# Turning the second group's queries on TensorE at the head of a fused attention and ELU kernel

## The chip, the cores and the metric

The kernel runs on one core of a Trainium2 chip. The metric is the time of one execution in microseconds, as the median over several runs. A core has a matrix engine (TensorE, PE in the profile, with its weight loads shown apart as PEld), a vector engine (VectorE, DVE), a scalar engine (ScalarE, ACT), a general engine (GpSimd, POOL) and a queue engine that issues most DMAs (SyncE, SP). Each engine works through its own instructions in order and waits on semaphores for the others.

## The reference

Everything is float32. The first part is an attention with a polynomial feature map, the second a two-layer network with an ELU:

```python
# q, k, v: (4, 4, 1088, 32); S1, S2: (8, 32)
def phi(x):
    a = np.einsum('rd,bhsd->bhsr', S1, x)
    b = np.einsum('rd,bhsd->bhsr', S2, x)
    return np.einsum('bhsi,bhsj->bhsij', a, b).reshape(*x.shape[:-1], 64)
q_p, k_p = phi(q), phi(k)
kv = np.einsum('bhsf,bhsd->bhfd', k_p, v)
z = np.sum(k_p, axis=2)
num = np.einsum('bhsf,bhfd->bhsd', q_p, kv)
den = np.einsum('bhsf,bhf->bhs', q_p, z)[..., None] + 1e-06
x = (num / den).transpose(0, 2, 1, 3).reshape(4352, 128)

# w_in: (128, 2048), w_out: (2048, 128)
h = x @ w_in
g = np.where(h > 0.0, h, np.exp(np.minimum(h, 0.0)) - 1.0)
out = g @ w_out
```

## The kernel before

**Tiles and groups.** A batch has 17 tiles of 64 tokens, so there are 68 in all. Eight tiles make a group, g = 0 to 8. Group 0 is tiles 0 to 7 of batch 0, group 1 is tiles 8 to 15 of batch 0; tile 16 of batch 0 belongs to group 2. `x` of a group lies transposed in SBUF as `xg` (128 features by 512 tokens). The network's 2048 middle columns are taken in eight chunks cp of 256. For each pair (g, cp), `mm1` makes `h` in two halves, `elu_a` (ACT) and `elu_d` (DVE) turn it into `gg`, and `mm2` adds up the output. Groups 2 to 7, and the last chunks of group 1, use a scheme of seven products in place of eight for `mm2` (`sums7` on POOL, `mm2_seven` on PE); it isn't touched.

**Loads.** Inputs arrive as pairs of 32-bit words, and the weights are rounded on the chip to float32 by the steps RA, RB, RC (RS, RM, RD) and RE, all of which are on DVE but RB, which is on ACT (line 106). RC_2 does RS, RM and RD of the first two blocks at once. The queries of a batch come into `hd_q` with heads and 32 token groups on the partitions. For batch 0 they come in two DMAs, tiles 0 to 7 and tiles 8 to 16.

**The head.** The program is written out by hand in the order in which every engine is to see its instructions (`manual_schedule`). The head brings the first group to `mm1`:

- `transp` (line 281, DVE) turns blocks of 32 by 32 of `hd_q` or `hd_k` into `qT` or `kT`, where the feature dimension is on the partitions.
- `KF`, `KO_pool` and `KO_first` make the key features, `KA` (line 428) adds up `kv` over the tiles. `KS_first` copies `kv` twice side by side (kd, ACT), turns it on PE, and copies the result to `kvS` (ACT).
- `q1_first`, `q1z_first`, `q2_den` and `q2_out` make the first group's query features `qp` on DVE, with RA(0) and RA(1) in between.
- `q4_early` (line 636) turns `qp` on PE in two halves of two heads, through PSUM tiles `qtp`, and ACT copies each half into `qpT` (line 637).
- `q1_second` (line 537) multiplies the second group's `qT` with `SW`, which holds the two feature matrices and the sums z; ACT copies the result into `abw` (line 541), and q2(1) later makes the second group's features from it.
- `q5_early` (line 643) multiplies `qpT` with `kvS` in 16 small tiles into two PSUM tiles `xps`, one for each half w of the token columns; ACT copies them into `xg` (line 649).
- `mm1_first` (line 857) does the first `mm1` column half by column half, so that it can start when the first of the two copies is there.
- `keep_warm` issues matmuls on constants whose result nobody reads.

Matmuls with fewer than 128 output columns sit in parts of the array; `tile_position` says which. A float32 matmul shows in the profile as two records. PSUM tiles come from rings: `h` has four banks, `aux` two, `o0` and `o1` one each.

After the head, a loop over `steps` runs `mm1`, the ELU and `mm2` of a step two back. Other work is hung onto steps by `at` (behind `mm1`), `mid` and `late` (behind the ELU).

## Time and profile before

| | |
|---|---|
| median of 3 runs | 265.38 us (265.32 to 265.83) |
| the profiled execution | 265.08 us |
| its span, first to last instruction | 263.3 us |
| TensorE's granted clock | 1.000 |
| DMA in the first 25 us | 176 to 349 GB/s in most slices |
| stretch 0 to 9.40 us | PE busy 8.29, DVE 6.67, ACT 3.11 |
| stretch 9.40 to 15.55 us | PE busy 5.16, DVE 5.73, ACT 3.62 |
| stretch 15.55 to 18.30 us | PE busy 2.72, DVE 2.65, ACT 1.64 |

The profile is one execution. Times in it count from the first instruction. A row of a timeline reads: start, length, engine, line, operation, output and inputs, shapes, count, and in brackets the idle time before it and what ended that. A row with a count covers several instructions, from the first one's start to the last one's end. Rows of the chain read: start, length, what.

### The profile page before, as it was taken

The numbers are of one execution on the slowest core, as the hardware profiler recorded it, in microseconds if no ns is written. First come the engines' busy times: TensorE is split into PE (matmuls) and PEld (weight loads), VectorE is DVE, ScalarE is ACT, GpSimd is POOL, SyncE is SP. The second block draws the span as 40 slices with busy tenths as digits, with TensorE's granted clock in tenths as the row PEclk, the third lists the DMA queues.
The fourth block names the chain that finished last, engine by engine and source line by source line (L and its number), as shares of the span: only waits on it lengthen the run. The fifth ranks groups of instructions, "written<-read, shape, count | busy, mean of one in ns | idle before, by whom it ended". The sixth has DMA issues, their size and how long they took to land.

```text
span 263.3 us, 9739 instructions
## 1 busy us (share of the span) xinstructions
PE 257.8 (98%) x4127; PEld 160.5 (61%) x4127; DVE 188.2 (71%) x349; ACT 184.5 (70%) x356; POOL 168.2 (64%) x251
## 2 busy tenths in 40 slices
PE   8899999999999999999999999999999999999994
PEld 7652334354346756667666666665666666667994
DVE  6899999997969997996477676644446445674651
ACT  2479978677567656775587777776777777777793
POOL 4400009105477996798869799888688888998300
PEclk9999999999999999999999999999999999999999
DMA  5997099020011110000100110011001100110011
GB/s 176 339 349 209 2 277 230 1 72 18 2 24 26 26 20 2 2 4 17 31 3 0 29 18 0 2 19 25 3 2 21 23 4 0 18 20 8 2 30 32
DMA packets 26442, 13.73 MB, mean 52 GB/s; under 512 B 19328, under 2 KB 24576, under 8 KB 26400
## 3 DMA queue, kind: packets, MB, share of 16 engines
q1 hardware_dynamic: 25968, 12.76, 18.9%
q8 instruction: 32, 0.52, 0.9%
q10 hardware_dynamic: 368, 0.30, 0.3%
q0 software_dynamic: 64, 0.07, 0.1%
q14 instruction: 10, 0.08, 0.1%
HBM read 10.88 MB, written 2.23 MB: 50 GB/s over the span
## 4 chain that ended last, share of the span: by engine, by line
PE 96%; POOL 1%; DVE 1%; ACT 1%; issue 0%
PE h L257 44%; PE pb L792 16%; PE pa L792 13%; PE o L257 5%; PE pb L768 4%; PE ol L257 3%; PE idle L265 1%; PE kv L428 1%; PE h L686 1%; PE qps L686 1%; POOL kp L324 1%; PE kfps L360 1%; PE qps L576 1%; PE qtp L636 1%; PE kv L257 1%; PE abp L341 1%
## 5 line engine op out<-in xcount | busy, mean ns | idle before, releaser
L257 PE MATMUL h<-xg,W 128*32 128x512 f32 (+3 forms) x904 | 130.7, 539 | 0.4 <-ACT xg L649 0.4
L875 DVE SCALAR_TENSOR_TENSOR gg<-e,h 128x512 f32<-128x512 f32 x128 | 85.6, 683 | 54.1 <-ACT e L869 50.6
L867 ACT ACTIVATE e<-h 128x512 f32<-128x512 f32 x128 | 75.5, 590 | 45.6 <-PE h L257 42.9
L869 ACT ACTIVATE e<-e 128x512 f32<-128x512 f32 x128 | 80.9, 632 | 3.8
L257 PEld LDWEIGHTS h<-xg,W 128*32 128x32 f32 (+1 forms) x904 | 42.6, 122 | 43.2 <-issue 34.9
L754 POOL TENSOR_TENSOR tt<-gg 128x256 f32<-128x256 f32 x50 | 37.0, 741 | 16.4 <-DVE gg L875 16.1
L751 POOL TENSOR_TENSOR tt<-gg 128x256 f32<-128x256 f32 x50 | 36.7, 734 | 5.5 <-DVE gg L875 5.1
L755 POOL TENSOR_TENSOR tt<-tt,gg 128x256 f32<-128x256 f32 x50 | 37.5, 750 | 3.9
L756 POOL TENSOR_TENSOR tt<-gg,tt 128x256 f32<-128x256 f32 x50 | 37.2, 744 | 3.9
L792 PEld LDWEIGHTS pa<-gg,W 128*64 128x64 f32 (+1 forms) x496 | 23.8, 125 | 23.5 <-issue 22.9
L792 PE MATMUL pa<-gg,W 128*64 128x128 f32 (+1 forms) x496 | 30.5, 274 | 0.0
L792 PE MATMUL pb<-tt,SS 128*64 128x128 f32 (+1 forms) x480 | 29.5, 273 | 0.0
L792 PEld LDWEIGHTS pb<-tt,SS 128*64 128x64 f32 (+1 forms) x480 | 22.6, 126 | 0.0
L792 PE MATMUL pa<-tt,SS 128*32 128x128 f32 (+1 forms) x288 | 21.0, 273 | 0.0
L133 POOL TENSOR_TENSOR raw<-raw,tiny 128x512 f32<-128x512 f32 x1 | 1.0, 1044 | 29.4 <-DVE raw L128 29.4
L792 PE MATMUL pb<-tt,W 128*64 128x128 f32 (+1 forms) x256 | 19.8, 273 | 0.0
L792 PE MATMUL pb<-gg,SS 128*64 128x128 f32 (+1 forms) x256 | 19.8, 273 | 0.0
L257 PE MATMUL o<-gg,W 128*32 128x512 f32 x128 | 15.3, 594 | 0.0
L792 PEld LDWEIGHTS pa<-tt,SS 128*32 128x32 f32 (+1 forms) x288 | 13.6, 124 | 0.0
L792 PEld LDWEIGHTS pb<-gg,SS 128*64 128x64 f32 (+1 forms) x256 | 12.7, 125 | 0.0
L792 PEld LDWEIGHTS pb<-tt,W 128*64 128x64 f32 (+1 forms) x256 | 12.6, 125 | 0.0
L768 PE MATMUL pb<-gg,W 128*32 128x256 f32 x192 | 11.5, 380 | 0.0
(163 smaller groups left out, 279.5 us busy)
## 6 DMA issues: line engine op xcount, KB each, us to landing
raw<-in_moe_w_in_dram SPq DMA_DIRECT2D x8, 256.0 KB, 6.6
raw<-in_moe_w_out_dram SPq DMA_DIRECT2D x8, 256.0 KB, 6.4
hd_k<-in_k_dram SPq DMA_DIRECT2D x3, 544.0 KB, 7.3
hd_q<-in_q_dram SPq DMA_DIRECT2D x3, 544.0 KB, 7.9
out_dram<-ob SPq DMA_DIRECT2D x88, 16.0 KB, 1.5
v<-in_v_dram SPq DMA_DIRECT2D x4, 288.0 KB, 6.8
v<-in_v_dram SPq DMA_DIRECT2D x4, 256.0 KB, 8.3
hd_k<-in_k_dram SPq DMA_DIRECT2D x1, 288.0 KB, 3.3
```

Source lines behind the costliest of these rows:

```text
L257: nc.tensor.matmul(dst[c:c + tile], lhs[:, c:c + tile], rhs, skip_group_check=True, tile_position=(0, c), **kw)
L265: nc.tensor.matmul(idle[c:c + tile, :cols], ones[:, :tile], ones[:, :cols], skip_group_check=True, tile_position=(0, c))
L686: nc.tensor.matmul(ps[w][s * r:s * r + s, 64 * k:64 * (k + m)], lhs, qpT[g, i][rows, o + 2 * k:o + 2 * (k + m), f, :], start=(f == 0 and j ...
L751: nc.gpsimd.tensor_tensor(t[:, 0], b12, b11, op=SUB)
L754: nc.gpsimd.tensor_tensor(t[:, 2], b22, b12, op=SUB)
L755: nc.gpsimd.tensor_tensor(t[:, 1], t[:, 2], b11, op=ADD)
L756: nc.gpsimd.tensor_tensor(t[:, 3], b21, t[:, 1], op=SUB)
L768: nc.tensor.matmul(acc[1][0][r:r + width[0], 256 * hi:256 * hi + 256], lhs[:, w:w + width[0]], gg[:, c, 256 * u:256 * u + 256], start=(cp ...
L792: nc.tensor.matmul(bank[r:r + width[0], P * col:P * col + P], lhs[:, w:w + width[0]], rhs[:, u], start=(first and i in ((0,) if g == 1 els ...
L867: nc.scalar.activation(e, hs[g, cp][c][:, :n], RELU, scale=-1.0)
L869: nc.scalar.activation(e, e, EXP, scale=-1.0)
L875: nc.vector.scalar_tensor_tensor(gs[g, cp][:, c, :n], es[g, cp][:, c, :n], -1.0, hs[g, cp][c][:, :n], op0=ADD, op1=MAX)
```

## The change

DVE no longer turns the second group's queries in one instruction between the first group's features and the rounding of the weights. Instead `turn_q` multiplies each 32 by 32 block with the identity on PE, in four tiles on the diagonal of the array, and `turn_q_out` copies the result on ACT to `qT`. This happens in two batches of four query tiles behind `KA`, in one PSUM bank, with the first part of `KS_first` in between. Tile 16 is still turned by DVE, behind step 3 of the loop. RB(0) moves ahead of `KA`; RB(1) stands behind the second copy. `KS_first`'s copy to `kvS` moves into `q4_early` between its two halves. `q1_second` is split into three parts: one between the halves of `q4_early`, one between the two pairs of heads of `q5_early`, and one behind them. Its copy to `abw` stands between the two copies to `xg`. The second `xps` tile of group 0 comes from the ring of `h` in place of `aux`. One `keep_warm` goes, another shrinks from 192 columns to 64.

```diff
--- before.py
+++ after.py
@@ -281,6 +281,23 @@
         nc.vector.transpose(dst[b][:, t0:t1, :].rearrange("p t (a c) -> p c t a", c=2), hd[x, b][:, :, t0:t1, :])
 
 
+
+    def turn_q(t0, t1):
+        if not turned_q:
+            turned_q.append(psum.tile([P, 512], F32, name="qtu", tag="h", bufs=4))
+        for t in range(t0, t1):
+            for c in range(2):
+                for h in range(H):
+                    r = slice(D * h, D * h + D)
+                    o = 64 * (t - 8) + 32 * c
+                    nc.tensor.matmul(turned_q[0][r, o:o + 32], hd["q", 0][r, c, t, :], ident[r, r],
+                                     skip_group_check=True, tile_position=(D * h, D * h))
+
+    def turn_q_out(t0, t1, copy=nc.scalar.copy):
+        copy(qT[0][:, t0:t1, :].rearrange("p t (a c) -> p t a c", c=2),
+             turned_q[0][:, 64 * (t0 - 8):64 * (t1 - 8)].rearrange("p (t c a) -> p t a c", c=2, a=32))
+
+    turned_q = []
     SXh = const.tile([P, FD], F32, name="SXh")
 
     def make_SXh():
@@ -475,10 +492,12 @@
             z_tile(0, ps, i)
         return ps, ZC(0, ps)
 
-    def KS_first():
+    def KS_first_a():
         kd = work.tile([P, 2, R * R], F32, name="kd", tag="kd", bufs=1)
         nc.scalar.copy(kd[:], _ap(kv_ps[0][:, :R * R], [[0, 2], [1, R * R]]))
         nc.tensor.transpose(kv_ps[0][:, 128:256], kd[:].rearrange("p w f -> p (w f)"), ident[:])
+
+    def KS_first_b():
         nc.scalar.copy(kvS[:].rearrange("p h d -> p (h d)"), kv_ps[0][:, 128:256])
 
     def KV_first():
@@ -529,14 +548,21 @@
                                  qT[b][:, t, :], SW[:, :, 2, :], skip_group_check=True, tile_position=(0, 64 * u))
         return p[:, :128].rearrange("p (t h r) -> p h t r", t=4, h=H)
 
-    def q1_second():
-        p = psum.tile([P, 512], F32, name="abwp", tag="h", bufs=4)
-        for i in range(4):
+    second = []
+
+    def q1_second(i0, i1):
+        if not second:
+            second.append(psum.tile([P, 512], F32, name="abwp", tag="h", bufs=4))
+        p = second[0]
+        for i in range(i0, i1):
             for u in range(2):
                 b, t = half_tile(1, 2 * i + u)
                 nc.tensor.matmul(p[64 * u:64 * u + 64, i * 96:i * 96 + 96], qT[b][:, t, :],
                                  SW[:].rearrange("p h x r -> p (h x r)"), skip_group_check=True,
                                  tile_position=(0, 64 * u))
+
+    def q1_second_out():
+        p = second[0]
         abw[1] = work.tile([P, H * 4, 3 * R], F32, name="abw1", tag="abq1", bufs=1)
         nc.scalar.copy(abw[1][:].rearrange("p (h t) y -> p h t y", h=H),
                        p[:, :384].rearrange("p (t h y) -> p h t y", t=4, h=H))
@@ -624,7 +650,7 @@
             nc.vector.tensor_mul(qp[g][:, h], _ap(a_, list(a_.ap[1:]) + [[0, R]]),
                                  _ap(b_, [b_.ap[1], [0, R], b_.ap[2]]))
 
-    def q4_early(g):
+    def q4_early(g, between=None):
 
         qpT[g] = work.tile([P, H, 2, P], F32, name="qpT", tag="qpT", bufs=2)
         for hh in range(2):
@@ -635,18 +661,32 @@
                     r = (2 * hh + h2) * 4 + 2 * m
                     nc.tensor.transpose(p[:, o:o + P], qp[g][:, r:r + 2].rearrange("p t i j -> p (t i j)"), ident[:])
             nc.scalar.copy(qpT[g][:, 2 * hh:2 * hh + 2], p[:].rearrange("p (h m s) -> p h m s", h=2, m=2))
+            if between and hh == 0:
+                between()
 
     def q5_early(g):
-        xp = [psum.tile([P, 512], F32, name="xps", tag="aux") for _ in range(2)]
-        for h in range(H):
+        q5_early_a(g, range(H))
+        q5_early_b(g)
+
+    def q5_early_a(g, hs_):
+        if 0 in hs_:
+            xps[g] = [psum.tile([P, 512], F32, name="xps", **kw) for kw in
+                      (dict(tag="aux"), dict(tag="h", bufs=4) if g == 0 else dict(tag="aux"))]
+        xp = xps[g]
+        for h in hs_:
             for w in range(2):
                 nc.tensor.matmul(xp[w][D * h:D * h + D, :256], kvS[64 * w:64 * w + 64, h, :],
                                  qpT[g][64 * w:64 * w + 64, h].rearrange("p m s -> p (m s)"),
                                  skip_group_check=True, tile_position=(64 * w, D * h))
+
+    def q5_early_b(g, between=None):
+        xp = xps.pop(g)
         xg[g] = work.tile([P, 512], F32, name="xg", tag="xg", bufs=3)
         to = xg[g][:].rearrange("p (m w s) -> p w m s", w=2, s=P)
         for w in range(2):
             nc.scalar.copy(to[:, w], xp[w][:, :256].rearrange("p (m s) -> p m s", s=P))
+            if between and w == 0:
+                between()
 
 
     def heads(g):
@@ -965,19 +1005,24 @@
     zq = q1z_first()
     q2_den(0, zq, lambda: RA(0))
     q2_out(0, 2, lambda: RA(1))
+    RB(0)
     KA(0)
-    KS_first()
-    keep_warm(1)
-    RB(0)
+    turn_q(8, 12)
+    KS_first_a()
+    turn_q_out(8, 12)
+    turn_q(12, 16)
+    turn_q_out(12, 16)
     RB(1)
-    q4_early(0)
-    transp(qT, "q", 0, 8, NT)
+    q4_early(0, lambda: (KS_first_b(), q1_second(0, 1)))
     RC_2()
     RE(0)
     RE(1)
-    q1_second()
-    q5_early(0)
-    keep_warm(1, 192, width[0])
+    q5_early_a(0, (0, 1))
+    q1_second(1, 3)
+    q5_early_a(0, (2, 3))
+    q1_second(3, 4)
+    q5_early_b(0, q1_second_out)
+    keep_warm(1, 64, width[0])
     mm1_first()
     q2(1, 2, lambda: RA(2))
     RB(2)
@@ -1065,6 +1110,7 @@
         late(n_a, sums_out, b)
         at(n_z, turn, b)
         late(n_z, turned, b)
+    late(3, transp, qT, "q", 0, 16, NT)
     late(10, transp, qT, "q", 1, 0, NT)
     at(21, transp, qT, "q", 2, 0, NT)
     late(24, transp, qT, "q", 3, 0, NT)
```

## The prediction

> **What bounds the kernel now.** I read the page's busy shares first, then its chain of waits, then the same chain in order of time for the first 50 us, and last the timeline and single tiles there.

> ```profile
> PE 257.8 (98%) x4127; PEld 160.5 (61%) x4127; DVE 188.2 (71%) x349; ACT 184.5 (70%) x356; POOL 168.2 (64%) x251
> ...
> PE 96%; POOL 1%; DVE 1%; ACT 1%; issue 0%
> ```

> TensorE is busy 98% of the span and carries 96% of the chain: whatever starts its dense part later makes the kernel that much longer. The chain in order of time shows where the dense part starts (start, length, what):

> ```profile
> 11.01 0.69 DVE qp L624
> 11.70 0.21 DVE W L101
> 11.91 0.61 DVE qp L624
> 12.52 0.14 issue
> 12.65 0.63 PE qtp L636 x4
> 13.28 0.85 PE abwp L537 x16
> 14.13 0.70 PE xps L643 x16
> 14.83 0.64 ACT xg L649 x2
> 15.47 0.11 issue
> 15.58 2.79 PE h L257 x40
> ```

> From 15.58 (`mm1_first`) on only PE rows follow. So the change is worth what it does to 15.58, plus what its side effects do soon after. The timeline of that stretch (start, length, engine, line, tiles, count, idle before):

> ```profile
> 7.50 0.16 PEld L419 LDWEIGHTS zps<-abk 128*32 128x32 f32 x8 [0.22 <-ACT abk L349]
> 9.43 1.21 PE L428 MATMUL kv<-kp,v 128*32 128x64 f32 x72
> 10.71 0.27 ACT L480 COPY kd<-kv 128x128 f32<-128x128 f32 x1 [1.90 <-PE kv L428]
> 11.55 0.91 ACT L106 ACTIVATE W<-W,ebias 128x256 uint32<-128x256 uint32 x2
> 12.42 0.77 DVE L281 STREAM_TRANSPOSE qT<-hd_q 128x576 f32<-128x576 f32 x1
> 12.45 0.59 ACT L637 COPY qpT<-qtp 128x512 f32<-128x512 f32 x1
> 13.31 0.59 ACT L637 COPY qpT<-qtp 128x512 f32<-128x512 f32 x1 [0.28 <-PE qtp L636]
> 14.18 0.48 ACT L541 COPY abw<-abwp 128x384 f32<-128x384 f32 x1 [0.27 <-PE abwp L537]
> 15.01 0.76 DVE L136 SCALAR_TENSOR_TENSOR W<-raw,W 128x256 f32<-128x256 f32 x2
> ```

> Two strands meet at 15.58. One is x: `qpT`, `xps`, then `xg`, whose first pair of columns is copied by about 15.18. The other is W: DVE's transposition (12.42 to 13.19), then RC_2, then RE(0), whose first instruction ends at 15.43. PE takes 0.115 us from a DVE end to a load behind two waits (12.50 to 12.62 at the second `qtp`), so 15.43 + 0.115 is 15.55, where the load of `h` stands. The chain names ACT, but x had been there for 0.3 us: W came last. Taking 0.77 us off DVE there looks like a gain.

> [...] here records of different tiles start 7 ns apart (below). [...] the pair at 11.55 overlaps by 0.10 (two of 0.51 and 0.50 in 0.91).

> **The change part by part.** *Turning.* One `turn_q` call issues 4 tiles x 2 x 4 = 32 matmuls, and an f32 matmul is two records (KA: 36 matmuls, 72 records), so 64, on four tiles of the array at a time. Not in the trace; bounds: eight loads of 0.109 in 0.16 us start 7 ns apart, so at least 64 x 7 ns = 0.45; KA's 72 records with twice the columns take (1.21 - 0.22) / 72 = 13.8 ns each, so at most 0.88. I take 8 ns, 0.51, near the lower end since half as many columns stream, and add the 0.20 that one record of 32 columns lasts (`zps`, 196 ns): 0.71. Changing the tile's shape costs PE the stream of the last record and about 0.09 (last `abwp` record at 13.88, first `xps` at 14.06: 96 columns at 0.84 ns, then 0.09; last `qtp` to `h`: 0.2 for 128 columns).

> *The new order*, with 0.05 from an engine's end to the next engine's start (kd to its transposition: 10.98 to 11.03):

> - PE: KA's last record starts at 10.42; `turn_q(8, 12)` 10.57 to 11.28. Its data, the second half of the first `hd_q`, completes in the trace at 10.39, so 0.18 is spare; SP's queue is unchanged there. kd's transposition follows at 11.2.
> - ACT: RB(0) moves to 10.2 to 10.7, where ACT was idle 1.90 us: free. kd is copied to 10.98 as before. First copy-out, 128x256 from PSUM, 0.37 (like `abq` and `xg`): 11.33 to 11.70.
> - PE: `turn_q(12, 16)` writes the bank that this copy reads, so it waits: 11.75 to 12.46. Queued behind it on PE are `qtp` and all that x needs. ACT: second copy 12.51 to 12.88.
> - ACT: RB(1), now behind this copy, 12.78 to 13.29 (before: ended 12.46). DVE's RC_2 waits for RB(1): 13.35 instead of 13.12. The removed 0.77 us become 0.85 us of waiting; RE(0) ends at 15.67, 0.24 later.
> - PE: first `qtp` four 12.38 to 13.04 (before 11.76 to 12.41), first part of `q1_second`, second `qtp` four 13.27 to 13.90.
> - ACT: `qpT` 13.19 to 13.78, kvS to 13.94, `qpT` to 14.53 (before 13.90).
> - PE: first two heads of x from 13.99, their second records 0.24 later; `q1_second(1, 3)` 14.56; last two heads 15.04 to 15.68. In before, x ended at 14.72. Two shape switches, 0.3 each with the streams, lie in front of the last heads: features between the heads aren't free.
> - ACT: first `xg` copy 15.75 to 16.12; `abw` copy to 16.51; second `xg` copy to 16.79, in time for `mm1_first`'s second half (16.17 + 4 x 0.215 = 17.03).
> - PE: `mm1_first` at 16.17: **+0.59**.

> *After that.* q2(1) on DVE waits for `abw`: 16.57 instead of 15.68, +0.89. Its `qp` ends at 19.22; the second `qtp` four of the second group would want it at 19.38: just hidden. But DVE runs without a break from 17.03 to 22.9, so RE(2), which ended at 20.73, ends 0.82 later, and mm2(0, 0) starts at 21.60 instead of 20.91. That makes +0.69. Beyond, DVE rounds and ELUs have 0.8 us or more before PE needs them (RE(3) ends at 23.84 for 26.09), so it neither grows nor is won back.

> *Costed at nothing*: the smaller `keep_warm`s (they fill PE's idle time; no cover needed); tile 16's transposition at step 3 (0.2 us like other small ones, in DVE's slack behind 26; without that, +0.2); `hd_q`'s later release (the load that reuses it is issued at 34.73, after step 3 near 28; SP's later loads stand behind it); the fifth to eleventh `h` tiles (their readers are done by then); POOL has no part.

> **Sum**: +0.7. The profiled execution took 265.08 us (span 263.3 and 1.8 around it), so it would be about 265.8; the median of the runs is 265.38, 0.3 higher, so **266.1**.

> **Unknown costs.** Turning: 0.45 to 0.88 each, -0.1 to +0.74 for both, since the two are in line. Bank wait: 0, if hardware order allowed it, to the 0.42 taken; without it -0.35. Shape switches: hidden to as priced, -0.35 to 0. DMA: if the half landed with w_out's delay of 6.4 instead of 5.8, 10.95, +0.4; I take 10.39.

> **Rivals.**
> 1. *Little change*: second turn isn't held by the first copy, or switches overlap; x is then +0.0 to +0.35, and W +0 (RB(1) at 12.94 at the latest). For: PE had 1.1 us of idle time between 10.64 and 11.76. About 265.6.
> 2. *Turning at KA's rate*: +0.7 + 0.74, 266.8. For: the tiles stay loaded only 32 columns, and each needs its own weight load. Against: loads run ahead.
> 3. *Faster*: DVE's freed time is used. RC_2 could start at 12.56, when `qp` ends, so W could be ready at 15.0: -0.55, 264.8. It decides where the second copy-out ends by 12.1, so that RB(1) ends by 12.5, and x is out of PSUM by 15.0. For: W is the last strand today. Against: the second copy waits for turn, copy, turn in sequence; even at 7 ns a record it ends at 12.8.
> 4. *Clock*: with less warming PE drops to a lower clock for some us, +1 to +2. Against: PEclk is 9 in all slices and PE's longest new gap is about 0.6 us.

> **Chances.** Forecast 0.55 (0.10 of it under the bound), rival 1 0.16, rival 2 0.17, rival 3 0.08, rival 4 0.04. A difference under 0.2%, 0.53 us, can't be told from none. So slower 0.45 + 0.17 + 0.04 = 0.66, same 0.26, faster 0.08. The forecast's own range is 265.6 to 266.6; with rivals 1 and 2 most of the way, 265.2 to 267.0.

> **What would show it.** In the profile after: 64 `qtu` records a call in about 0.7 us; the second batch starting 0.05 behind the first copy's end at about 11.7; RC_2's first instruction waiting on ACT `W` near 13.3; `xg` ending near 16.1 and 16.8; `h` starting at 16.2 and `o` at 21.6. It is wrong if `qtu` is one unbroken batch, if RB(1) ends by 12.5, or if `h` starts by 15.6.

## The result, and the profile after

The changed kernel takes **271.58 us** (median; 271.34 to 272.18) against 265.39 for the kernel before on the same chip: ratio 1.0231, 95% interval 1.0214 to 1.0247. The sign was forecast, the size was not: +6.2 us where +0.7 was expected, far above the range's upper end of 267.0. Of the 6.2 us only about 0.5 came by the way that was forecast (few_records, below). The profiled execution spans 270.0 us, 6.7 more than before.

The rows of the page (busy time and share, chain by engine, granted clock in 40 slices of 6.75 us):

```profile
span 270.0 us, 9994 instructions
PE 261.9 (97%) x4253; PEld 162.9 (60%) x4253; DVE 188.0 (70%) x349; ACT 185.4 (69%) x358; POOL 168.3 (62%) x251
PEclk9959999999999999999999999999999999999999
PE 95%; issue 1%; DMA 1%; ACT 0%; DVE 0%; SPq 0%; DVEq 0%
```

PE has 126 matmul records more: 128 of the two turning calls, less 2 of the `keep_warm` that went. As many weight loads come with them (PEld, x4253 against x4127). Two things are new. "issue" has 1% of the chain, and in the third slice the clock stands at 5, half speed. The chain of waits in order of time (start, length, what) shows both:

```profile
9.68 1.21 PE kv L445 x72
10.89 0.53 PE qtu L293 x37
11.42 3.14 issue
14.56 0.56 PE qtu L293 x21
15.12 0.02 issue
15.14 0.38 ACT qT L297
15.52 0.04 issue
15.57 1.07 PE qtu L293 x64
16.64 1.04 PE qtp L662 x4
17.69 0.52 PE abwp L560 x4
18.21 1.05 PE qtp L662 x4
...
22.23 2.70 PE h L257 x40
```

In the middle of the first turning call PE does nothing for 3.14 us, and no semaphore is behind it: "issue" is time in which the engine waited for nothing that the profile shows. The timeline gives the same in records:

```profile
10.86 0.56 PE L293 MATMUL qtu<-ident,hd_q 32*32 32x32 f32 x43
14.56 0.54 PE L293 MATMUL qtu<-ident,hd_q 32*32 32x32 f32 x21 [3.14 <-issue]
15.57 1.07 PE L293 MATMUL qtu<-ident,hd_q 32*32 32x32 f32 x64
22.14 2.79 PE L257 MATMUL h<-xg,W 128*32 128x256 f32 x40
```

43 of the call's 64 records run, then the engine stops between two instructions of one kind, on one tile, with its inputs there (the call's queries came in one DMA). The second call of 64 takes 1.07 us, and the `qtp` fours take 1.04 and 1.05 in the chain instead of 0.63. The windows of that time (start:end, length, busy us and count of PE, PEld, DVE, ACT, POOL, then the granted clock, DMA share, GB/s) say why:

```profile
10.81:14.23 3.42, 0.61 (x50) 0.48 (x43) 1.78 (x4) 0.29 (x2) 0.00 (x0) 1.00 1.08 372
14.23:17.64 3.41, 3.01 (x92) 2.26 (x92) 0.12 (x1) 1.15 (x3) 0.00 (x0) 0.50 1.08 374
17.64:21.05 3.41, 3.41 (x28) 1.82 (x28) 2.46 (x5) 1.34 (x3) 0.00 (x0) 0.50 1.08 276
21.05:24.47 3.42, 3.42 (x62) 1.68 (x60) 1.83 (x6) 2.30 (x6) 0.00 (x0) 1.00 1.01 288
```

Behind 3.42 us in which PE was busy for only 0.61, the clock is at half for 6.83 us. `h` starts at 22.14 instead of 15.58, 6.56 late, and the span is 6.7 longer: nearly all of the loss lies ahead of `h`.

### The profile page after: what moved, and what is told of

Same layout as the page of the kernel before. It is cut to its first block, busy times and chain, and to the rows that moved or that the text cites. A ratio compares the mean times of both kernels' runs of the same rounds, so it can differ in the third digit from the quotient of the medians.

```text
span 270.0 us, 9994 instructions
## 1 busy us (share of the span) xinstructions
PE 261.9 (97%) x4253; PEld 162.9 (60%) x4253; DVE 188.0 (70%) x349; ACT 185.4 (69%) x358; POOL 168.3 (62%) x251
## 4 chain that ended last, share of the span: by engine, by line
PE 95%; issue 1%; DMA 1%; ACT 0%; DVE 0%; SPq 0%; DVEq 0%
PE h L257 43%; PE pb L832 16%; PE pa L832 13%; PE o L257 5%; PE pb L808 4%; PE ol L257 3%; PE kv L445 2%; DMA hd_k<-in_k_dram 1%; PE h L726 1%; PE qtp L662 1%; PE qps L726 1%; PE xps L678 1%; PE qtu L293 1%; PE abp L358 1%; PE kfps L377 1%
## 5 line engine op out<-in xcount | busy, mean ns | idle before, releaser
L257 PE MATMUL h<-xg,W 128*32 128x512 f32 (+3 forms) x904 | 130.7, 540 | 0.0
L257 PEld LDWEIGHTS h<-xg,W 128*32 128x32 f32 (+1 forms) x904 | 42.4, 122 | 42.8 <-issue 34.9
L794 POOL TENSOR_TENSOR tt<-gg 128x256 f32<-128x256 f32 x50 | 37.0, 741 | 16.2 <-DVE gg L915 15.9
L832 PEld LDWEIGHTS pa<-gg,W 128*64 128x64 f32 (+1 forms) x496 | 23.8, 125 | 23.5 <-issue 22.9
L257 PE MATMUL o<-gg,W 128*32 128x512 f32 x128 | 15.3, 594 | 0.0
L832 PEld LDWEIGHTS pb<-gg,SS 128*64 128x64 f32 (+1 forms) x256 | 12.6, 125 | 0.0
```

The costliest lines, as they stand in the source:

```text
L257: nc.tensor.matmul(dst[c:c + tile], lhs[:, c:c + tile], rhs, skip_group_check=True, tile_position=(0, c), **kw)
L794: nc.gpsimd.tensor_tensor(t[:, 2], b22, b12, op=SUB)
L832: nc.tensor.matmul(bank[r:r + width[0], P * col:P * col + P], lhs[:, w:w + width[0]], rhs[:, u], start=(first and i in ((0,) if g == 1 els ...
```

## The theories

**The theory: PE ran out of instructions.** The page has a DMA queue for instructions, q8. These are its rows (packets, MB, share), first before, then after:

```profile
q8 instruction: 32, 0.52, 0.9%
q8 instruction: 33, 0.54, 0.9%
```

In the trace each of its packets has 16,384 bytes (what a packet brings is called a block below), and the kernel with more PE instructions has one packet more: 32 for 8,254 loads and matmuls before, 33 for 8,506 after. The first packet of the span runs from 12.06 to 13.16 us in this kernel, and PE goes on 1.4 us behind it. Counting PE's loads and matmuls from the start, the stop comes after record 442. The kernel before reaches its 442nd record at 14.35 and starts its 443rd at 14.65, in the first of these rows (the second is from few_records, an experiment below):

```profile
14.65 0.16 PEld L265 LDWEIGHTS idle<-const-float32-1.0 128*32 128x32 f32 x8 [0.41 <-issue]
14.48 0.51 PEld L558 LDWEIGHTS abwp<-SW,qT 128*64 128x64 f32 x8 [0.41 <-issue]
```

The 0.30 us between the two records of before aren't a stop: the same 0.30 lies behind `xps` in few_records, where record 442 is still to come. So before, the next block of instructions came in time, though not by much: its 443rd record starts 1.56 us behind the end of the packet. Each turning call adds 64 loads and 64 matmul records in some 0.5 us, and PE comes to the end of the instructions at hand 3.1 us earlier (record 442 at 11.23 instead of 14.35), while the packet ends when it did before (13.16 against 13.09).

**The rivals.** Something in the turning itself holds PE: its data, its PSUM bank, or the array's tiles. Or the new order costs more than was worked out, and the clock with it. A second question was why the block comes so late: because PE asks late, or because the DMA engines are full (372 GB/s in the window of the stop).

## The experiments

Each kernel differs from the kernel after, or from the kernel before where that is said. "Stop" is the time from the start of record 442 (443 in the kernel with 32 dummies) to that of the next. Some expectations speak of the 449th, which is the same place with PE's drain and semaphore instructions counted too.

| kernel | median us, ratio (95%) | record 442 | next | stop | half clock | `h` starts |
|---|---|---|---|---|---|---|
| before | 265.39 | 14.35 | 14.65 | 0.30 (no stop) | none | 15.58 |
| after | 271.58, 1.0231 (1.0214 to 1.0247) | 11.23 | 14.56 | 3.33 | 6.83 | 22.14 |
| few_records | 265.90, 1.0015 (1.0005 to 1.0025) | 14.80 | 14.80 | 0 | none | 16.22 |
| dve_turn | 266.54, 1.0045 (1.0030 to 1.0060) | 16.20 | 16.20 | 0 | none | 16.42 |
| dummies16 | 266.40, 1.0038 (1.0023 to 1.0054) | 13.46 | 14.57 | 1.12 | none | 16.57 |
| dummies32 | 269.97, 1.0173 (1.0153 to 1.0193) | 11.09 | 14.57 | 3.48 | 3.41 | 20.00 |
| early_records | 272.71, 1.0279 (1.0210 to 1.0348) | 10.86 | 14.69 | 3.83 | 2 x 3.41 | 23.48 |
| late_loads | 267.75, 1.0097 (1.0080 to 1.0114) | 11.48 | 12.53 | 1.05 | none | 17.82 |
| lean_late | 268.37, 1.0109 (1.0084 to 1.0134) | 11.11 | 12.56 | 1.45 | 3.41 | 18.59 |
| lean_few | 265.88, 1.0018 (1.0011 to 1.0026) | 14.67 | 14.72 | 0.05 | none | 15.61 |

**few_records: the same order and copies, few instructions.** Each turning call is 4 matmuls of 256 columns that bring `hd_q` over unturned; the turning is left out.

```diff
-        for t in range(t0, t1):
-            for c in range(2):
-                for h in range(H):
-...
-                    nc.tensor.matmul(turned_q[0][r, o:o + 32], hd["q", 0][r, c, t, :], ident[r, r], ...)
+        for h in range(H):
+            r = slice(D * h, D * h + D)
+            o = 64 * (t0 - 8)
+            nc.tensor.matmul(turned_q[0][r, o:o + 256].rearrange("p (c t d) -> p c t d", c=2, d=D), ident[r, r],
+                             hd["q", 0][r, :, t0:t1, :], ...)
```

> The changed kernel with each turn call cut to 4 matmuls of 256 columns (16 records of PE in all in place of 128, 16 loads in place of 128): the same waits, copies and order, but it copies the queries unturned, so the turning is left out. Theory A (PE ran out of fetched instructions: it stood 3.14 us in the middle of the first turn call, at its 449th load or matmul record, and the half clock followed from that): no stop of over 0.3 us before h, clock 1.000, h starts near 16.1 instead of 22.1, time 265.8 to 266.4, which is what the prediction's sum gave for the order alone. Theory B (the order, the two copies and the smaller keep-warm work cost the time, and the clock falls because PE is warmed less): 270 or more, clock under 1.

265.90 us, no stop, full clock. Its timeline:

```profile
10.61 0.63 PE L291 MATMUL qtu<-hd_q,ident 32*32 32x256 f32 x8
11.74 0.63 PE L291 MATMUL qtu<-hd_q,ident 32*32 32x256 f32 x8 [0.23 <-ACT qT L295]
13.25 0.69 DVE L116 SCALAR_TENSOR_TENSOR W<-raw,W 128x512 uint32<-128x512 uint32 x1 [0.71 <-ACT W L106]
16.22 2.79 PE L257 MATMUL h<-xg,W 128*32 128x256 f32 x40
```

The calls take 0.63 us each, close to the 0.71 of the forecast, with the same data, bank, tiles and copies, so this is the forecast's schedule without its instructions: `h` at 16.22 (forecast 16.17). The stop is not the bank, the data or the order, and the clock does not fall from the smaller `keep_warm` work, which is the same here. That the stop hangs on the number of instructions is not yet shown: the small matmuls themselves are gone too.

**dve_turn: the new order, DVE turns the queries as before.**

```diff
-    turn_q(8, 12)
     KS_first_a()
-    turn_q_out(8, 12)
-    turn_q(12, 16)
-    turn_q_out(12, 16)
     RB(1)
+    transp(qT, "q", 0, 8, NT)
...
-    late(3, transp, qT, "q", 0, 16, NT)
```

> The changed kernel with DVE turning the queries again behind qp (one transposition of tiles 8 to 16, as before), all else as changed: RB(0) early, kvS late, features in three parts between the pairs of heads, keep-warm work cut. Theory A: no stop, clock 1.000, about 265.9: the first part of the features waits for DVE at 13.2 between the halves of q4, which costs 0.5. Theory B: 268 or more, since its order and keep-warm cuts stay.

266.54 us, no stop. The new order has its own cost here: `q1_second`'s first part stands between the halves of `q4_early` and waits for DVE's `qT`, and the second `qtp` four waits behind it.

```profile
13.36 0.39 PE L560 MATMUL abwp<-SW,qT 128*64 128x96 f32 x4 [0.92 <-DVE qT L281]
13.67 0.66 PE L662 MATMUL qtp<-ident,qp 128*128 128x128 f32 x4
```

That four started at 12.65 before, so it is 1.0 late, and `h` 0.84. In this order the turning on PE would be the better choice if its instructions came in time (few_records is 0.6 us faster); the order alone already loses to the kernel before.

**dummies16 and dummies32: the kernel before, with matmuls of constants behind KA.** 16 or 32 matmuls of 32 by 32 whose inputs are the identity and whose result nobody reads: no data, no `qtu` bank, no new order, only instructions. (32 is what one turning call has.)

```diff
     KA(0)
+    for i in range(32):
+        r = slice(D * (i % 4), D * (i % 4) + D)
+        nc.tensor.matmul(idle[r, :32], ident[r, r], ident[r, r], ...)
     KS_first()
```

> The kernel before with 16 matmuls of 32x32 on constants behind KA, that nobody waits for (64 records and loads). Theory A: PE reaches the 449th record 64 earlier in the program, near 13.1, and stands until about 14.6, when the next instructions are there as in both runs; +1 to +2 us. Theory B: PE is idle there anyway; +0.2 at most.

> The same with 32 matmuls (128 records and loads, as many as one turn call). Theory A: a stop of about 3 us inside these matmuls or just behind them, from about 11.3 to 14.6, the clock at a half for some us behind it, +4 to +6 us. Theory B: +0.4 at most.

With 32 the stop of the kernel after is back, at the same place within a group of 64 records and to the same end. With 16 it comes later in the program, on quite another instruction, and ends at the same time:

```profile
10.71 0.57 PE L971 MATMUL idle<-ident 32*32 32x32 f32 x43
14.57 0.38 PE L971 MATMUL idle<-ident 32*32 32x32 f32 x21 [3.29 <-issue]
...
15.49:18.90 3.41, 3.41 (x33) 2.85 (x39) 2.45 (x5) 2.00 (x5) 0.00 (x0) 0.50 1.09 379
```

```profile
14.57 0.69 PEld L537 LDWEIGHTS abwp<-SW,qT 128*64 128x64 f32 x16 [1.08 <-DVE W L116]
```

The first fence is dummies32 (timeline, then a window), the second dummies16's timeline, where the trace puts the stop down to DVE. The program gives no ground for that releaser: `abwp` reads nothing that RC_2 on DVE makes, RC_2's instruction (line 116) had ended at 14.22, 0.35 us before, and the row lies at the same record and the same time as the other stops. PE stops at the same count, on whatever instruction, until 14.57. Its queue also holds a drain and some semaphore instructions (seven in all ahead of the stop of the kernel after); with these counted, both stops and that of the kernel after stand behind PE's 449th instruction. This shows that the number of instructions is the cause. dummies16 also shows a stop without loss of clock: `h` starts 0.99 us later and the kernel is 1.0 us longer.

**early_records: 36 more records long before the head.** The first three `keep_warm` matmuls become twelve narrow ones.

```diff
-    keep_warm(3)
+    keep_warm(3, 256, 32)
```

> The changed kernel with the three first keep-warm matmuls of 128x128 issued as twelve of 128x32 (18 more records and 18 more loads before 4 us, same work). Theory A (a fixed number of PE instructions, 442 loads and records, is at hand until the next block of instructions has been fetched): the stop moves 18 records forward in the first turn call, to behind some 25 of its 64 instead of 43, again behind the 442nd. If the fetch is asked for when a given number of instructions is used up, it ends a little earlier than 14.56 too, by up to 0.9. Time 271 to 272. Theory B (something in the turn call or its data stops PE): the stop stays behind record 43.

```profile
10.65 0.40 PE L293 MATMUL qtu<-ident,hd_q 32*32 32x32 f32 x25
14.69 0.54 PE L293 MATMUL qtu<-ident,hd_q 32*32 32x32 f32 x39 [3.64 <-issue]
...
21.80 0.41 PE L560 MATMUL abwp<-SW,qT 128*64 128x96 f32 x5 [1.58 <-issue]
```

The stop moves from behind 43 matmul records of the call to behind 25, so the 36 loads and matmuls more ahead of it leave it at record 442. Its end does not come earlier (14.69 against 14.56): with the loads running, PE's using up instructions earlier didn't bring the block earlier. A second stop of 1.82 us comes behind record 697. With drain and semaphore instructions that is the 705th, 256 behind the 449th, and the packet ahead of its end runs from 18.87 to 20.26. The 272.71 us are the middle of two executions, 274.27 and 271.14; the trace is that of the longer one, so whether the shorter had the second stop isn't known.

**late_loads: the DMA engines are left free for the fetch.** All loads behind the second block of w_in are held back until `kd` is copied, by a small ACT write into the buffer that the first of them fills.

```diff
     load_w(1, 0)
-    load_w(1, 1)
-    load_w(0, 1)
-    for b in range(1, B):
-...
+    def late_loads():
+        load_w(0, 1)
+        load_w(1, 1)
+        for b in range(1, B):
+...
         nc.scalar.copy(kd[:], _ap(kv_ps[0][:, :R * R], [[0, 2], [1, R * R]]))
+        nc.scalar.copy(raw_2[:, 0, 2 * P, :].bitcast(F32), kd[:, 0, :2])
+        late_loads()
```

> The changed kernel with all loads behind the second weight block's w_in issued only after kd's copy on ACT (near 11 us, by one small ACT write into the tile that the next load fills), so that the DMA engines run empty near 11 us. Theory A1 (the instruction fetch is slow because it shares the DMA engines with 340 to 390 GB/s of data): PE goes on by 12.5 instead of 14.56, the clock stays at 1.000 or falls for a shorter time, 266 to 268.5. Theory A2 [...]: still a stop until about 14.5, and 271 or more.

```profile
12.53 0.38 PE L294 MATMUL qtu<-ident,hd_q 32*32 32x32 f32 x21 [0.86 <-issue]
13.39 0.75 PE L294 MATMUL qtu<-ident,hd_q 32*32 32x32 f32 x64 [0.22 <-ACT qT L298]
...
10.19:13.60 3.41, 2.33 (x161) 1.90 (x153) 2.75 (x8) 1.34 (x4) 0.58 (x4) 1.00 0.17 44
```

With 44 GB/s in place of 372 the packet runs from 10.11 to 11.22, 1.95 us earlier, PE goes on at 12.53, 2.03 earlier, and the clock stays whole. So the loads made the block late here, and A2, by which it would come as late with the DMA engines left free, is out. The packet itself takes 1.1 us in both kernels; it is its start that comes late. In each of the six kernels that stop, PE goes on 1.3 to 1.5 us behind the packet's end; what happens in that time no record shows. 267.75 us: still slower than before. 1.05 us of stop is left, the order keeps its 0.64, and in the profiled execution the first call starts 0.5 later than in few_records (11.11 against 10.61): the clock rose to full at 6.78 us in late_loads, at 4.21 in few_records.

**lean_late: the same, with an order in which ACT's copies hold up less.** RB(1) ahead of the second copy-out, `kvS` between the copies, the four heads of x in one go, the second group's features behind them.

```diff
     turn_q_out(8, 12)
+    KS_first_b()
     turn_q(12, 16)
-    turn_q_out(12, 16)
     RB(1)
-    q4_early(0, lambda: (KS_first_b(), q1_second(0, 1)))
+    turn_q_out(12, 16)
+    q4_early(0)
...
-    q5_early_a(0, (0, 1))
-    q1_second(1, 3)
-    q5_early_a(0, (2, 3))
-    q1_second(3, 4)
+    q5_early_a(0, range(H))
+    q1_second(0, 4)
```

> The same late loads, and the order mended as the first runs suggest: kvS copied between the two copies of the turned queries, RB(1) ahead of the second copy (ACT was idle there), x in one go with the features behind it. With A1 and no stop left: RC_2 starts near 12.6, h near 15.3, 265.1 (from 264.8 if nothing is late behind it to 266 if a late weight load or a short stop remains). With A2: 271.

A miss: 268.37. Three things are in its trace. The stop stays (1.45 us). The clock falls for 3.41 us. And RC_2, which reads only blocks of w_in, waits by the trace for a held-back load of w_out into the same buffer `raw_2`:

```profile
14.38 0.69 DVE L116 SCALAR_TENSOR_TENSOR W<-raw,W 128x512 uint32<-128x512 uint32 x1 [1.73 <-DMA raw<-in_moe_w_out_dram]
16.30 0.76 DVE L136 SCALAR_TENSOR_TENSOR W<-raw,W 128x256 f32<-128x256 f32 x2
...
10.95:14.36 3.41, 1.93 (x129) 1.55 (x116) 1.67 (x4) 1.47 (x6) 0.00 (x0) 1.00 0.52 157
14.36:17.78 3.42, 3.42 (x28) 1.74 (x28) 2.57 (x5) 1.52 (x4) 0.00 (x0) 0.50 0.94 280
```

The third, a side effect of the hold, costs nothing at `h`: RE(0)'s two instructions run from 16.30 to 17.06, and `h` follows at 18.59 behind PE's own work. For the other two lean_few (next) has the same order without stop and at full clock: against it the first `qtp` starts 1.82 later (14.10 against 12.28), behind the stop, and from there to `h` it takes 1.16 longer, most of it under half clock. This version gives no verdict on the order.

**lean_few: the leaner order with few instructions.** The two edits of few_records and lean_late's order together, all loads as before; the turning is left out.

> The kernel after with each turning call in 4 matmuls of 256 columns (the turning itself is left out: the columns come over unturned) and the order mended where few_records was late: RB(1) ahead of the second copy-out, kvS copied between the two copies, the four heads of x in one go and the second group's features behind them. It asks what this order would be worth if TensorE's instructions came in time. Theory A (the stop is from the instruction supply, 24 records in place of 128 stay under the limit): no stop, clock 1.0; W is then ready by RE(0) at about 15.0 and x's first xg copy at about 15.1 to 15.2, h starts at 15.2 to 15.4, 0.2 to 0.4 before the kernel before: 265.0 to 265.3, ratio 0.998 to 1.000. Rival (the two waits for the copies on the qtu bank cost as much as DVE's transposition saved, whatever the order): h at 15.6 to 16.0, 265.4 to 265.8, ratio 1.000 to 1.002.

265.88 us, a miss of the theory's 265.0 to 265.3 and 0.08 above its rival's range. Nothing stops, the clock is whole, but `h` is at 15.61:

```profile
12.28 1.09 PE L660 MATMUL qtp<-ident,qp 128*128 128x128 f32 x8
13.61 1.13 PE L676 MATMUL xps<-qpT,kvS 64*32 64x256 f32 x16 [0.24 <-ACT qpT L661]
14.66 0.88 PE L558 MATMUL abwp<-SW,qT 128*64 128x96 f32 x16
15.47 0.32 PE L265 MATMUL idle<-const-float32-1.0 128*32 128x64 f32 x8
15.61 2.77 PE L257 MATMUL h<-xg,W 128*32 128x256 f32 x40
```

W was ready at about 14.8 (RE(0)'s first instruction started at 14.40), 0.6 us sooner than before. It gains nothing: PE is in the way, with 0.88 of the second group's features and a `keep_warm` between x and `h`. Before, these features ran at 13.25 to 14.13, while x waited for its copies. So even with instructions in time, moving the turning off DVE moves the wait in this order from W to PE's own queue. The rest of the 0.47 us comes behind `h`: the first `o` is 0.11 later than before and the span 0.4 longer; where that arises wasn't followed. No kernel that beats the kernel before was run, nor one with these features behind the first `h`.

## Why the prediction was wrong, point by point

**What bounds the kernel: right.** Whatever starts `h` later makes the kernel that much longer: +6.56 at `h`, +6.7 in the span; in few_records +0.64 and +0.8.

**The cost of a turning record: nearly right, and not what mattered.** In late_loads the second call runs at full clock and without a stop: 64 records in 0.75 us, 8.9 ns apart; 0.71 and 8 were taken. The 1.07 us in the kernel after lie under half clock (14.23 to 21.05). The step that failed is this one: "One `turn_q` call issues 4 tiles x 2 x 4 = 32 matmuls ... so 64, on four tiles of the array at a time." They were priced by what the array takes. Each record also brings a weight load, so a call is 128 instructions on PE's queue, and PE stopped behind the 449th on that queue until 1.4 us after the end of a packet. That term was not in the sum, nor in its unknown costs. It measured 3.14 us of standing still, and the half clock behind it another 2.8 (below).

**The rest of the sum: right.** In few_records each step can be read at its place: second call 0.06 behind the first copy (forecast 0.05), RC_2 at 13.25 (13.35), `xg` to 16.16 and 16.86 (16.12 and 16.79), `h` at 16.22 (16.17), `o` at 21.55 (21.60), the whole 265.90 (266.1). This is the forecast's order with calls of 0.63 us. With the 0.75 of late_loads for each of the two calls it would be 266.1, an estimate from these two runs, so the forecast would have come out had the instructions been there.

**Rival 4, the clock: it fell, but not for the reason given.** The rival named less warming, and few_records has the same smaller `keep_warm` work at full clock, so that the clock was named at all is luck. "PE's longest new gap is about 0.6 us" held only without the stop. The size, +1 to +2, was too small: half clock for 6.83 us.

**How 6.56 us at `h` come about:** about 0.64 from the order (few_records), 3.14 of PE standing still in the stop, and the remaining 2.8 from the half clock. The last is a difference and takes in what else changed with the calls; 6.83 us at half speed lose at most 3.41.

**Rival 1** fell: that the second call waits for the first copy was the author's estimate, and it did wait (15.51 to 15.57). **Rival 2** fell too (8.9 ns a record, not 13.8). **Rival 3**, the faster one, named the point from which it decides: a second copy-out that ends by 12.1. It ended at 12.81 in few_records. lean_few took the copy out of W's way and had RB(1) done by 12.45, and still gained nothing: the rival's other condition, x out of PSUM by 15.0, wasn't met, as the second `xg` copy ended at 16.34.

What the profile before could have told: its q8 packets were on page and trace, and the first ends at 13.09. Nothing on the page says that PE was near its limit: where the instructions at hand end showed only in the kernels that stopped there. Looking back, dummies32 goes on 1.30 us behind its packet's end, and before was at that place 1.56 us behind it, so it had some 0.26 us to spare (an estimate from these two figures). The change put some 250 loads and matmuls more ahead of that place.

## What to carry to other kernels

Count instructions, not only array time, where a change replaces one instruction of another engine by dozens of small matmuls on PE: in float32 each 32 by 32 block was two loads and two matmul records, and 442 records were there until the next block came, about 14.6 us into this kernel. Where the loads fill the DMA engines, look for late instructions as well (here by 1.95 us, at 372 GB/s against 44). A gap put down to "issue" in the midst of equal instructions, with an instruction packet ending shortly before its end (here 1.3 to 1.5 us), points to this; the test is to add instructions that do nothing and see whether the stop moves to the same count.

## What the runs showed of the hardware

**When the clock falls.** It isn't the length of the stop alone: a stop of 3.33 us was followed by 6.83 us of half clock (after), stops of 3.48 and 3.83 by 3.41 each (dummies32 and the first stop of early_records), one of 1.45 by 3.41 (lean_late), those of 1.05 and 1.12 by none (late_loads, dummies16). In the kernel after the clock changed at 3.99, 14.23 and 21.05 us, 10.24 and 6.83 us apart, three times and twice the 3.41 that half clock lasted in dummies32. In stretches of 3.41 us counted from the clock's rise to full, PE busy for 1.83 us (54%, early_records) and 1.93 (57%, lean_late) was followed by half clock, 2.18 (64%, dve_turn) and 2.33 (68%, late_loads) were not. dve_turn's stretch, with the clock of the next one in the second row:

```profile
11.27:14.68 3.41, 2.18 (x21) 1.23 (x21) 3.34 (x7) 1.58 (x4) 0.00 (x0) 1.00 1.08 368
14.68:18.10 3.42, 3.42 (x64) 1.94 (x64) 2.29 (x8) 1.96 (x6) 0.00 (x0) 1.00 1.08 377
```

Whether it matters where in such a stretch a stop falls wasn't tested. Nor does the busy share decide alone: in after PE was busy for 3.01 us, 88%, of the first 3.41 at half clock, and half clock went on, while in dummies32 it ended behind 3.41 us in which PE was busy throughout. Why half clock lasted 6.83 us in the kernel after and in dummies32, with a stop as long, only 3.41 is not shown.
